# Retention attention and a two-layer MLP on one core: how the weights and the waves are loaded, and in which order two waves are computed

## Chip, cores and metric

The kernel runs on one core of a Trainium2 chip. The metric is the device time of one execution in microseconds (us). Times within the profile are counted from the start of its span. TensorE (PE) does matmuls, VectorE (DVE) and ScalarE (ACT) elementwise work, GpSimd (POOL) memsets and copies between SBUF tiles; SyncE (SP) issues DMAs, in order.

## What is computed

```python
# q, k, v: (4, 8, 768, 64) f32; lam: (8,); w_in: (512, 2048); w_out: (2048, 512); block = 64
for b in range(nb):                     # blocks of 64 positions
    intra = (qb @ kb.T) * Dmask         # Dmask[i, j] = lam ** (i - j) for i >= j, else 0
    intra = intra @ vb
    inter = (qb * lam_pow) @ kv_state   # lam_pow = lam ** (pos + 1)
    out[:, :, sl] = intra + inter
    kv_state = lam_block * kv_state + (kb * rev_pow).T @ vb
x = out.transpose(0, 2, 1, 3).reshape(3072, 512)
h = x @ w_in
g = h * (1 / (1 + exp(-1.702 * h)))
return g @ w_out                        # (3072, 512) f32
```

## The kernel before

**Waves.** The 768 positions are cut into six waves of 128. A wave holds 128 positions of all four batches, 512 rows, and all eight heads (four pairs). For each wave there is attention (with a state that goes on to the next wave), layer 1 (`mlp1`, L352: 16 blocks of 128 hidden columns, each four matmuls over the 512 model columns, followed by a `gelu` on ScalarE), and layer 2 (`mlp2`, L374: four groups of 128 rows, each 16 matmuls in four steps of `CW` = 4, followed by a copy to SBUF and a store). Matmuls are in bf16.

**Attention of waves 0 and 1** goes by units: one batch `b` and four heads `g`, eight units in all. `u_cast_kq` (L194) scales k and q by powers of lam into bf16, k on VectorE and q on GpSimd; `u_cast_v` (L208) casts v. `u_turn` (L222) transposes k and q on TensorE, `u_turn_copy` (L229) copies them from PSUM, `u_score` (L240) and `u_mask` (L249) make the masked scores, `u_out` (L278) makes the output and ScalarE copies it to `xT`, the input of layer 1; `u_kv` (L257) and `u_kv_up` (L265) update the state. **Attention of waves 2 to 5** goes by head pairs (`p_cast` L293, `p_score`, `p_mask`, `p_kv`, `p_out` L333), with the transposes done by DMAs from SyncE.

**PSUM.** The big matmuls share three buffers (`mm`); turns, outputs and states have one buffer each, scores one of two banks. Two units therefore follow each other through the same buffers.

**Loads.** q, k and v come by SyncE: `load_unit` (L78) fetches one of k, q, v of one unit, 128 KB in runs of 256 bytes; `load_pair` (L86) fetches one of them for a head pair with two DMAs. They land in tiles of the pool `ld`, two buffers per tag. The weights come by GpSimd's queue with a cast from f32 to bf16 in the DMA (`load_w_in` L159, five DMAs; `load_w_out` L165, four DMAs). `sync_behind` (L172) is a tiny DMA on SyncE that reads from the second block of `w_out`; SyncE stands at it until that block has landed. Behind it stand the 24 loads of wave 1.

**Order.** The order of the work on every engine is that in which the program writes it (`manual_schedule`). Wave 0's attention is a loop over units with three units in flight; it issues the first `w_in` load from its sixth and seventh steps. Then come all other weight loads, `sync_behind`, and wave 1's loads. After it, `main` is the list of layer-1 blocks and layer-2 steps, and `side` a list of the other pieces, each with a position in `main` before which it is written. The order of `main` is: layer 1 of wave 0, layer 2 of wave 0, then for batches 0 and 1 of wave 1 (half of its columns) layer 1 and layer 2, then the same for batches 2 and 3, then waves 2 to 5. `units1` (L480) puts wave 1's units of batches 0 and 1 into layer 2 of wave 0, with their state updates, and those of batches 2 and 3 into the work on the first half of wave 1. `full` (L514) puts wave w+1's attention into wave w's work; wave 2's lies in the second half of wave 1.

## Time and profile before

| | us |
|---|---|
| median of six runs | 225.42 |
| the six runs | 225.49, 225.97, 225.35, 223.42, 222.63, 226.01 |
| the profiled execution | 223.28 |
| its span, first to last instruction | 221.6 |
| TensorE busy in the span | 206.7 |
| VectorE, ScalarE, GpSimd busy | 92.1, 95.2, 35.2 |

TensorE's granted clock is 1.00 through the whole span. HBM reads are 27.27 MB, writes 6.29 MB. In the profile, a line of the timeline gives the start, the duration of a group of like instructions, the engine, the line of the kernel, the operation with output and inputs, how many there are, and in brackets the idle time ahead of it with what ended it. In a line of windows stand the stretch, its length, and for each of PE, PEld, DVE, ACT and POOL the busy time and number of instructions, then the granted clock, the busy share of the 16 DMA engines, and the GB/s they moved. The chain is the work that ended last, followed back from the last instruction.

### The profile page before, as it was taken

How to read it: one execution, taken by the hardware profiler on the slowest of the kernel's cores; microseconds unless marked ns; L12 is line 12 of the kernel's file. 1: busy time of each engine (PE TensorE's matmuls, PEld its weight loads, DVE VectorE, ACT ScalarE, POOL GpSimd, SP SyncE). 2: the span in 40 equal slices, each digit the busy share in tenths (PEclk: the TensorE clock that was granted, in tenths of full speed). 3: DMA queues.
4: the chain of work that ended last, by engine and by line, in shares of the span. 5: the costliest groups of instructions: out<-in, count | busy, mean ns of one | idle time of the engine just before them, and what ended most of it. 6: DMA issues, size and time to landing. Idle time of an engine off the chain costs nothing.

```text
span 221.6 us, 3886 instructions
## 1 busy us (share of the span) xinstructions
PE 206.7 (93%) x1476; PEld 108.6 (49%) x1476; DVE 92.1 (42%) x218; ACT 95.2 (43%) x202; POOL 35.2 (16%) x57
## 2 busy tenths in 40 slices
PE   7687999799999895999999999999999999999993
PEld 2354344356775584444455444554444545444452
DVE  0793000355688982182563183571363332100121
ACT  5986672273751363055612066511166411376000
POOL 4869300332121011011020120110120000000000
PEclk9999999999999999999999999999999999999999
DMA  5999999999999999889875999746792132200112
GB/s 128 238 217 145 207 206 214 218 234 218 202 215 289 190 236 134 184 240 167 195 161 140 211 250 192 179 108 187 185 264 49 27 94 71 95 3 0 47 47 95
DMA packets 109638, 35.91 MB, mean 162 GB/s; under 512 B 102324, under 2 KB 106676, under 8 KB 109620
## 3 DMA queue, kind: packets, MB, share of 16 engines
q1 hardware_dynamic: 105236, 31.47, 63.2%
q0 software_dynamic: 4240, 4.19, 12.0%
q8 instruction: 11, 0.18, 0.3%
q14 instruction: 7, 0.06, 0.1%
q10 hardware_dynamic: 144, 0.00, 0.0%
HBM read 27.27 MB, written 6.29 MB: 151 GB/s over the span
## 4 chain that ended last, share of the span: by engine, by line
PE 72%; DMA 14%; SPq 6%; DVE 2%; POOL 2%; issue 1%; ACT 0%; DVEq 0%; ACTq 0%
PE ps_out L379 32%; PE ps_h L358 29%; DMA w_out<-in_moe_w_out_dram 7%; SPq L82 5%; DMA qf<-in_q_dram 4%; PE ps_s L311 2%; DMA xT<-xs 2%; PE ps_o L337 2%; PE ps_out L397 2%; PE ps_o L339 2%; PE ps_kv L326 2%; POOL w_in L161 1%; DMA vf<-in_v_dram 1%; PE ps_t L227 1%; SPq L90 1%
## 5 line engine op out<-in xcount | busy, mean ns | idle before, releaser
L358 PE MATMUL ps_h<-xT,w_in 128*128 128x512 bf16 (+1 forms) x448 | 88.5, 349 | 1.5 <-DMA w_in<-in_moe_w_in_dram 1.5
L364 ACT ACTIVATE g_sb<-ps_h 128x512 bf16<-128x512 f32 (+1 forms) x112 | 59.5, 537 | 59.7 <-PE ps_h L358 58.7
L379 PE MATMUL ps_out<-w_out,g_sb 128*128 128x512 bf16 x368 | 84.6, 379 | 0.0
L358 PEld LDWEIGHTS <-w_in 128*128 128x128 bf16 x448 | 42.2, 98 | 38.7 <-DMA w_in<-in_moe_w_in_dram 2.1
L379 PEld LDWEIGHTS <-g_sb 128*128 128x128 bf16 x368 | 34.3, 98 | 37.3
L386 DVE COPY o_sb<-ps_out 128x512 f32<-128x512 f32 x19 | 13.1, 691 | 57.7 <-PE ps_out L379 50.2
L318 DVE TENSOR_TENSOR sm<-ps_s,dmask 128x512 bf16<-128x512 f32 x32 | 20.6, 686 | 26.9 <-PE ps_s L311 26.9
L300 POOL CAST v_sb<-vf 128x512 bf16<-128x512 f32 x16 | 11.4, 715 | 100.1 <-DMA vf<-in_v_dram 60.4
L342 ACT CAST xs<-ps_o 128x512 bf16<-128x512 f32 x16 | 9.4, 586 | 26.8 <-PE ps_o L339 23.2
L206 DVE TENSOR_TENSOR kqs<-kf,k_pow 128x256 bf16<-128x256 f32 x16 | 7.6, 477 | 26.8 <-DMA kf<-in_k_dram 22.5
L206 POOL TENSOR_TENSOR kqs<-qf,q_pow 128x256 bf16<-128x256 f32 x16 | 10.3, 648 | 28.7 <-DMA qf<-in_q_dram 26.0
L251 DVE TENSOR_TENSOR sm<-ps_s,dmask 128x512 bf16<-128x512 f32 x16 | 11.0, 689 | 3.7 <-PE ps_s L246 3.2
L329 DVE SCALAR_TENSOR_TENSOR kv<-kv,blk_pow,ps_kv 64x256 bf16<-64x256 bf16 x24 | 11.4, 476 | 0.2
L337 PE MATMUL ps_o<-kv,kq 128*128 128x128 bf16 x64 | 9.0, 220 | 2.4 <-ACT xs L342 2.4
L289 ACT CAST xT<-ps_o 128x256 bf16<-128x256 f32 x16 | 6.0, 374 | 9.7 <-PE ps_o L287 9.6
L339 PEld LDWEIGHTS <-sm 128*128 128x128 bf16 x128 | 7.9, 98 | 4.0 <-issue 2.6
L298 DVE TENSOR_SCALAR kqs<-kf,k_pow 128x256 bf16<-128x256 f32 x32 | 9.8, 348 | 0.2
L274 DVE SCALAR_TENSOR_TENSOR kv<-kv,blk_pow,ps_kv 64x64 bf16<-64x64 bf16 x32 | 7.7, 279 | 5.0 <-PE ps_kv L262 4.5
L298 DVE TENSOR_SCALAR kqs<-qf,q_pow 128x256 bf16<-128x256 f32 x32 | 9.7, 346 | 0.0
L227 PE MATMUL ps_t<-ident,kqs 128*128 128x128 bf16 x64 | 6.8, 221 | 2.8 <-DVE kqs L206 2.1
L211 ACT CAST v_sb<-vf 128x256 bf16<-128x256 f32 x16 | 6.4, 401 | 6.2 <-DMA vf<-in_v_dram 6.0
L339 PE MATMUL ps_o<-v_sb,sm 128*128 128x64 bf16 x128 | 9.0, 193 | 0.0
(54 smaller groups left out, 110.9 us busy)
## 6 DMA issues: line engine op xcount, KB each, us to landing
kf<-in_k_dram SPq DMA_DIRECT2D x48, 128.0 KB, 3.0
qf<-in_q_dram SPq DMA_DIRECT2D x48, 128.0 KB, 3.1
vf<-in_v_dram SPq DMA_DIRECT2D x48, 128.0 KB, 3.0
out_dram<-o_sb SPq DMA_DIRECT2D x23, 256.0 KB, 2.8
w_out<-in_moe_w_out_dram POOLq DMA_DIRECT2D x4, 512.0 KB, 15.8
w_in<-in_moe_w_in_dram POOLq DMA_DIRECT2D x3, 512.0 KB, 9.4
w_in<-in_moe_w_in_dram POOLq DMA_DIRECT2D x2, 256.0 KB, 5.8
kq<-kqs SPq DMA_TRANSPOSE x16, 3.5
```

The costliest lines, as they stand in the source:

```text
L82: nc.sync.dma_start(out=loaded[w, nm, b][:, 2 * g : 2 * g + 2, :, :].rearrange("s p h d -> s (p h) d"), in_=SRC[nm][b, 4 * g : 4 * g + 4, ...
L206: eng.tensor_tensor(out.rearrange("s p h d -> s (p h) d"), xf.rearrange("s p h d -> s (p h) d"), tab, op=MUL)
L298: nc.vector.tensor_scalar(kqs[:, i, :, h, :], loaded[w, "kq"[i], p][:, :, h, :], scalar1=(k_pow, q_pow)[i][:, 2 * p + h : 2 * p + h + 1], ...
L300: nc.gpsimd.tensor_copy(v_sb[w % 2][:, p, :, 0:3:2, :], loaded[w, "v", p])
L318: nc.vector.tensor_tensor(sm[:, h], s[:, h], dmask[:, h, p : p + 1, :].to_broadcast([P, B, P]), op=MUL)
L329: nc.vector.scalar_tensor_tensor(new[hd(h), p, :, hd(h)], old[hd(h), p, :, hd(h)], blk_pow[hd(h), 2 * p + h : 2 * p + h + 1], t[hd(h), :, ...
L337: nc.tensor.matmul(o[:, b, :], kq_of[w, p][:, 1, b, :], kv_sb[w % 2][:, p, b, :], start=True, stop=True)
L339: nc.tensor.matmul(o[:, b, hd(h)], sm[:, h, b, :], v_sb[w % 2][:, p, b, 2 * h, :], start=False, stop=True, skip_group_check=True)
L358: nc.tensor.matmul(t[:, bs[0] * P : bs[1] * P], w_in_sb[j][:, kc, i * P : (i + 1) * P], xT(w)[:, kc, bs[0] : bs[1], :].rearrange("p b t -> ...
L364: nc.scalar.activation(g_tile(w)[:, fc, c], h_ps.pop((w, fc))[:, c], GELU)
L379: nc.tensor.matmul(t, g_of[w][:, fc, g * P : (g + 1) * P], w_out_sb[j][:, fc % CW, :], start=(fc == 0), stop=(fc == FFC - 1))
L386: nc.vector.tensor_copy(o, t)
```

## The change

All f32 loads, the weights too, go through SyncE's queue into one ring of 26 slots of 256 KB (52 half slots; a unit load takes a half, a head pair or a weight block a whole). `coming` lists the loads in the order in which they will be used; `pump` issues those at its head as long as their slots are free in program order; `read` frees a slot. A weight block is 128 rows by 512 columns; VectorE casts it to bf16 (`cast_w`), 16 casts for `w_in` and 16 for `w_out`. The GpSimd weight loads, `sync_behind` and the pool `ld` go. The order of loads is: wave 0, `w_in`, half A of wave 1 (batches 0 and 1), `w_out`, half B (batches 2 and 3), wave 2.

The order of `main` becomes: layer 1 of wave 0, layer 1 of half A of wave 1, layer 2 of wave 0, layer 1 of half B, layer 2 of wave 1, then waves 2 to 5 as before. Half A's units lie in the last blocks of layer 1 of wave 0 (a unit every 1.3 blocks; v is cast on GpSimd, turns are copied by VectorE), half B's in layer 2 of wave 0 (every 2.2 steps; v cast and turns copied by ScalarE). The state updates of A and B are split off (`states1`) and come later: A's in layer 2 of wave 0, B's in layer 1 of half B. The casts of `w_out` are written behind A's units at every 0.6 of a position, so on VectorE 14 of them stand ahead of A's first state update and all 16 ahead of B's first cast. Wave 2's attention lies in layer 2 of wave 1.

```diff
+    NR = 26
+    ring = const.tile([P, 2 * NR, W // 2], f32, name="ring")
+    head, used, where, coming = [0], set(), {}, []
+    def load_w(kind, j, r):
+        def go(x):
+            if kind == "in":
+                src = moe_w_in[r * P : (r + 1) * P, j * W : (j + 1) * W]
+            else:
+                src = moe_w_out[(j * CW + r) * P : (j * CW + r + 1) * P, :]
+            nc.sync.dma_start(out=x, in_=src)
+            loaded[kind, j, r] = x
+        coming.append((2, (kind, j, r), go))
+    def pump():
+        while coming:
+            n, key, go = coming[0]
+            i = (head[0] + (n - 1) * (head[0] % 2)) % (2 * NR)
+            if any(c in used for c in range(i, i + n)):
+                break
+            used.update(range(i, i + n))
+            where[key] = (i, n)
+            head[0] = i + n
+            coming.pop(0)
+            go(ring[:, i : i + n, :].rearrange("s n c -> s (n c)"))
+    def read(*key):
+        i, n = where.pop(key)
+        used.difference_update(range(i, i + n))
+        return loaded.pop(key)
+    def cast_w(kind, j, r, eng):
+        eng.tensor_copy((w_in_sb if kind == "in" else w_out_sb)[j][:, r, :], read(kind, j, r))
...
+    A_UNITS = [(b, g) for g in range(NG) for b in range(HB)]
+    B_UNITS = [(b, g) for g in range(NG) for b in range(HB, B)]
+    for u in ROWS:
+        load_w("in", *u)
+    for u in A_UNITS:
+        for nm in "kqv":
+            load_unit(1, nm, *u)
+    for u in ROWS:
+        load_w("out", *u)
+    for u in B_UNITS:
+        for nm in "kqv":
+            load_unit(1, nm, *u)
+    load_full(2)
+    pump()
...
-        for j in range(1, len(IN_COLS)):
-            load_w_in(j)
-        for j in range(NJ):
-            load_w_out(j)
-        sync_behind(w_out_sb[1])
-        for u in UNITS:
-            for nm in "kqv":
-                load_unit(1, nm, *u)
+        for u in ROWS[2:]:
+            cast_w("in", *u, nc.vector)
+            pump()
...
+        for fc in range(3, FFC):
+            put(1, fc_whole, 0, fc)
+        units1(A_T, A_UNITS, A_S, nc.gpsimd, nc.vector)
+        for fc in range(3):
+            put(0.25, mlp1, 1, fc, [0, 1], HA)
+        for fc in range(3):
+            put(0.25, fc_rest, 1, fc, HA)
+        for fc in range(3, FFC):
+            put(0.5, fc_whole, 1, fc, HA)
+        for n, u in enumerate(ROWS):
+            at(13.2 + 0.6 * n, cast_w, "out", *u, nc.vector)
+        e = clock[0]
+        for j in range(NJ):
+            for g in range(3):
+                put(1, mlp2, 0, g, j)
+        for j in range(NJ):
+            put(1, mlp2, 0, 3, j)
+        states1(e + 0.5, A_UNITS, 2.2)
+        units1(e + 2, B_UNITS, 2.2, nc.scalar, nc.scalar)
+        e = clock[0]
+        for fc in range(FFC):
+            put(0.5, fc_whole, 1, fc, HB_)
+        states1(e + 1, B_UNITS, 1.9)
+        for g in range(G):
+            for j in range(NJ):
+                put(1, mlp2, 1, g, j)
+        full(e + 2, e + 8.3, 2, 2.4)
+        load_spread(e + 8, 3, 2)
```

`put` appends a piece to `main` at the running position and moves it on by its length; `at` appends to `side`.

## The prediction, on record before the changed kernel ran

> **What bounds the kernel now.** I read the page first, then TensorE's timeline from the end of wave 0's attention to the start of wave 2's layer 1, then SyncE's, then the windows for DMA rates. "Layer 1" is `mlp1`, "layer 2" is `mlp2`, a "unit" one batch and four heads of a wave.
>
> The page: busy time, and the chain of work that ended last.
>
> ```profile
> PE 206.7 (93%) x1476; PEld 108.6 (49%) x1476; DVE 92.1 (42%) x218; ACT 95.2 (43%) x202; POOL 35.2 (16%) x57
> ...
> PE 72%; DMA 14%; SPq 6%; DVE 2%; POOL 2%; issue 1%; ACT 0%; DVEq 0%; ACTq 0%
> ```
>
> TensorE holds 72% of the chain; DMA and SyncE's queue hold 20%, so at most some 44 us could be theirs, and the timeline says how much of it TensorE really loses.
>
> ```profile
> 18.29 0.27 PE L262 MATMUL ps_kv<-v_sb,kqs 128*128 128x128 bf16 x2
> 19.61 1.04 PE L358 MATMUL ps_h<-xT,w_in 128*128 128x512 bf16 x4 [1.04 <-DMA w_in<-in_moe_w_in_dram]
> ...
> 24.09 10.53 PE L358 MATMUL ps_h<-xT,w_in 128*128 128x512 bf16 x48 [0.41 <-DMA w_in<-in_moe_w_in_dram]
> 34.46 5.34 PE L379 MATMUL ps_out<-w_out,g_sb 128*128 128x512 bf16 x24
> 41.09 0.29 PE L227 MATMUL ps_t<-ident,kqs 128*128 128x128 bf16 x2 [1.29 <-DVE kqs L206]
> 41.59 0.29 PE L227 MATMUL ps_t<-ident,kqs 128*128 128x128 bf16 x2 [0.21 <-POOL kqs L206]
> ...
> 56.10 0.40 PE L227 MATMUL ps_t<-ident,kqs 128*128 128x128 bf16 x4 [0.53 <-DVE kqs L206]
> ...
> 87.41 0.22 PE L337 MATMUL ps_o<-kv,kq 128*128 128x128 bf16 x1 [2.41 <-ACT xs L342]
> ...
> 94.77 8.80 PE L358 MATMUL ps_h<-xT,w_in 128*128 128x512 bf16 x40
> ```
>
> The brackets are idle time. A matmul of 512 columns takes 0.216 us (48 of them fill 24.09 to 34.46). From 24.09 to 94.77 lie 240 such matmuls' worth (48 left of layer 1, 64 of layer 2, 128 for wave 1), 51.8 us; wave 1's eight units at 0.88 (turns 0.22, scores 0.22, outputs 0.33, states 0.11, the steps of the timeline) are 7.0; wave 2's attention is 4.45 (the steady waves start at 94.93 and 127.03 in the chain, 32.10 apart, less 27.65 for 128 matmuls). That is 63.3 of 70.7 us: **7.4 us are lost there**, 0.7 more between 19.61 and 24.09. After 94.77 TensorE has no hole to the end.
>
> SyncE's timeline shows the origin: it stands until the second block of `w_out` lands, and only then fetches wave 1.
>
> ```profile
> 12.29 1.61 SPq L82 DMA_DIRECT2D vf<-in_v_dram  x3
> 34.24 0.75 SPq L173 DMA_DIRECT2D behind<-w_out  x1
> 35.03 0.39 SPq L82 DMA_DIRECT2D kf<-in_k_dram  x1
> ```
>
> The windows (last two columns: DMA share, GB/s) give rates: loads of 256-byte runs, the casting weight loads, stores of 2 KB runs.
>
> ```profile
> 6.00:14.00 8.00, 5.89 (x63) 3.27 (x63) 7.03 (x15) 7.65 (x24) 6.10 (x9) 1.00 1.07 241
> 26.00:34.00 8.00, 8.00 (x38) 3.63 (x37) 0.00 (x0) 5.58 (x10) 0.00 (x0) 1.00 1.24 206
> 204.00:214.00 10.00, 10.00 (x48) 4.56 (x47) 1.38 (x2) 0.60 (x1) 0.00 (x0) 1.00 0.14 52
> ```
>
> **The one unknown: microseconds per weight row block of 256 KB (call it r).** The new loads are f32, 2 KB runs, on SyncE. Fast end: the casting loads write 206 GB/s of bf16, so read 412 GB/s of f32, r = 0.64. Slow end: 241 GB/s, r = 1.09. Nearest row: stores on the same queue with the same 2 KB runs, 52 / 0.14 = 371 GB/s at a full share, r = 0.70, which I take. SyncE's issue does not set it (0.33 to 0.45 us for a 256 KB store).
>
> **Part by part, with r = 0.70.**
>
> Start. SyncE's 24 loads of wave 0 stay as they are, to 13.9. A unit load lands 3.0 us after issue, and they run 0.55 apart, so weight row n lands at about 16.5 + 0.70(n+1): rows 0, 7, 15 at 17.2, 22.1, 27.7. VectorE is busy with wave 0 to 18.76 and then casts. A cast of 128x512 is not in the trace: L298's 0.347 us for half as many elements is the low bound, the 0.69 of L386 (512 elements from PSUM) the high one; I take 0.48, nearer L298, which reads SBUF. Rows 0 and 1 are cast at 19.7, where layer 1 started before (19.61): 0. Rows 2 and 3 at 20.7 (they were needed at 21.33), rows 4 to 7 at 22.7, and 16 matmuls end at 23.5. So block 1 starts at 23.5, not 24.09: **gain 0.6**. At 0.69 per cast it would be 24.3. Later blocks arrive every 2.8 us and are used every 3.46, so the casts stay hidden.
>
> Layer 1 with half A of wave 1. A's 12 loads follow at 0.55: the first unit's q lands at 28.8, GpSimd's 0.61 makes 29.4. TensorE reaches that unit's turn after 28 matmuls, 23.5 + 6.05 = 29.55: just in time. Units come every 1.65 us by load and every 2.0 by use. TensorE: 10.4 (48 matmuls) + 3.1 (four units at 0.77, states come later) + 6.9 (layer 1 of half A) = 20.4. New holes, since the first unit's score follows its turn without a matmul between (turn to score is 1.03 us at 7.62 to 8.65 in wave 0, less the turn's 0.22): 0.8; the fourth's score behind a turn and an output: 0.5; layer 1 of A right behind the last output, which needs a ScalarE copy (0.37 and hand-overs): 0.7. Plus 0.4 for the switches that the present units also show (four matmuls take 0.95 instead of 0.86 beside a score). Layer 2 starts at 46.3.
>
> Layer 2 of wave 0. `w_out` follows A (last landing 34.3) and is in at 45.5; its casts lie on an idle VectorE. A new order matters: VectorE's state updates of unit A0 stand behind 14 of the 16 `w_out` casts, and unit A1's state matmul (49.0) waits for them; row 13 lands at 44.1, plus 1.5 for cast and four updates: 45.6, hidden by 3.4 us. B's loads land from 46 to 52.1; its first turn is at 50.0, the fourth near 57. So 13.8 + 0.44 (states) + 3.1 (units) + 1.0 for holes and switches: 64.6. Its end carries no load wait.
>
> The rest. Second half of layer 1, 6.9 + 0.44: 72.0. Wave 2's loads land by 65.3, while its last cast comes at about 71; its transposes stand on SyncE behind wave 0's four stores, which are issued by 65. Layer 2 of wave 1 with wave 2's attention: 13.8 + 4.45 = 18.3: 90.3. Here 28 matmuls (6.0 us) follow the last output and cover its copy (0.59) and transpose (2.6): the 2.41 us hole goes. From wave 2's layer 1 on the order is that of before: 0.
>
> GpSimd loses the nine weight issues (6.9 us, off the path). Beside VectorE's f32 SBUF casts its own casts stretch (1.59 instead of 0.62 us at 163.06); two such stretches on its memsets (1.03 and 1.88) still end before 28.8: 0. SBUF writes grow by 4.2 MB; this is inside r.
>
> **Sum:** 94.77 - 90.3 = **4.5 us** less. The profiled execution took 223.28 (span 221.6 and 1.7 around it), so 218.8; the six runs lie in two bunches (222.63 to 223.42, 225.35 to 226.01), their median 225.42 is 2.1 above the profiled run and their mean is 224.8. I forecast from the mean, since this trace does not show what parts the bunches: **220.3**.
>
> A rule that speaks against the change. The row first: unit loads land 3.0 us after issue and still follow each other every 0.55 us, so the fixed cost of one overlaps the others, and the sum above goes by that. The Trainium skill, "DMA: Bandwidth & Descriptors", section Measured, asks for 1 MiB and more per DMA, and its fit gives each DMA 2.0 us plus its bytes at 436 GB/s. Taken one at a time, that is by estimate 2.6 us per row block, and by the stall formula of rival 1 a kernel some 30 us slower.
>
> **Rivals.**
>
> 1. *Slow loads (slower).* 2 KB loads run at the 241 GB/s of the unit loads. Every row later delays A: TensorE's stall at its first turn is 16(r - 0.70) - 0.15, at r = 1.09 6.1 us; row 13 of `w_out` then lands at 23.1 + 30r = 55.8, 57.3 with its updates, against 55.1: 2.2 more. 220.3 + 8.3 = **228.6**. It eats the whole gain from r = 0.99 (265 GB/s) on. For: loads have never run faster on this queue in the trace. Against: those were 256-byte runs, at SyncE's issue pace (128 KB per 0.55 us).
> 2. *Tight units (no change).* The spacing of A and B leaves one or no matmul block between a unit's dependent steps, and each of eight units loses the 0.81 us of turn to score: 6.5 instead of the 3.0 counted (2.0 in A, 1.0 in B): **223.8**. For: wave 0, so interleaved, takes 1.45 us per unit for 0.88 of work. Against: in A and B four matmuls stand between most of the steps.
> 3. *No holes.* All the 3.4 us of holes and switches counted in A and B hide: **216.9**. For: nothing is late by more than 0.8. Against: the orders named leave nothing to run in them.
>
> **How the numbers follow.** The forecast 0.60, with casts from 0.35 to 0.69, r from 0.64 to 0.85 (2.3 us at the top) and the two bunches, its own range 217.5 to 222.8; no holes 0.08; tight units 0.16; slow loads 0.16. About 1% is what a measurement of this kernel tells from no change: 223.2 to 227.7. Tight units fall below that line one time in eight (0.02). Faster 0.60 + 0.08 + 0.02 = 0.70; same 0.14; slower 0.16. The range 216.5 to 226.5 holds the forecast, tight units, half of no holes and a fifth of slow loads, about 0.83.
>
> **What would show it.** Right: weight rows landing about 0.7 us apart; TensorE's idle before the first A turn under 0.5 us; no DMA named in its waits after 24 us; layer 2 of wave 0 starting near 46, wave 2's layer 1 near 90; 32.1 us per wave after it. Wrong: row 15 landing after 30, a state matmul waiting for VectorE near 49, or later waves longer than 32.1, which would mean that the ring or the shared queue delays them.

## The result and the profile after

The changed kernel takes 226.80 us (median of 35 runs, 224.63 to 230.58) against 224.23 us of the kernel before (70 runs, 222.63 to 226.90): ratio 1.0096, 95% interval 1.0073 to 1.0118. It is about 1% slower; 220.3 was forecast. The profiled execution took 227.24 us, its span is 225.5 us. Executions that were over 1.5% above the fastest of the same kernel, most of them at a lower granted clock, are left out of every ratio (so 1.0096 is not 226.80 / 224.23), and of e1, e9, e11 and e16 only such an execution was profiled, so that their starts are missing in the table below and of e16 only the places of SyncE's work are read.

The page of the changed kernel, busy time and chain:

```profile
PE 209.8 (93%) x1476; PEld 110.2 (49%) x1476; DVE 106.9 (47%) x250; ACT 94.2 (42%) x198; POOL 30.8 (14%) x52
...
PE 79%; SPq 7%; DMA 6%; DVE 4%; issue 1%; ACT 1%; ACTq 0%; DVEq 0%
```

DMA fell from 14% of the chain to 6%, TensorE rose from 72% to 79%, and still the kernel is longer. A share of the chain says who was waited for last, not that time was saved. TensorE's timeline says where the time lies (changed kernel; start, duration, idle time ahead in brackets):

```profile
20.06 0.38 PE L386 MATMUL ps_h<-xT,w_in 128*128 128x512 bf16 x1 [0.56 <-ACT xT L317]
20.87 1.46 PE L386 MATMUL ps_h<-xT,w_in 128*128 128x512 bf16 x3 [0.43 <-DVE w_in L137]
...
31.98 0.39 PE L255 MATMUL ps_t<-ident,kqs 128*128 128x128 bf16 x4
...
48.76 1.03 PE L407 MATMUL ps_out<-w_out,g_sb 128*128 128x512 bf16 x4
...
66.73 1.04 PE L386 MATMUL ps_h<-xT,w_in 128*128 128x256 bf16 x8
...
93.65 0.81 PE L386 MATMUL ps_h<-xT,w_in 128*128 128x512 bf16 x3
95.89 8.14 PE L386 MATMUL ps_h<-xT,w_in 128*128 128x512 bf16 x37 [1.43 <-DMA xT<-xs]
...
110.46 0.40 PE L340 MATMUL ps_s<-kq 64*128 64x128 bf16 x8 [3.17 <-DVE sm L347]
111.34 0.38 PE L355 MATMUL ps_kv<-v_sb,kqs 128*128 128x128 bf16 x4 [0.48 <-DVE kv L358]
...
131.11 1.24 PE L386 MATMUL ps_h<-xT,w_in 128*128 128x512 bf16 x5
```

Wave 2's layer 1 starts at 93.65, 1.1 us earlier than before (94.77). But wave 2 then lasts to 131.11, 37.5 us instead of 32.1: it first waits for its own last `xT`, then for wave 3's first masks. So a gain of 1.1 is followed by a loss of 5.4, of which the three waits in brackets (1.43, 3.17 and 0.48) are 5.1. From wave 3 on the two kernels run alike.

Why the masks are late stands in VectorE's timeline of the changed kernel. The first lines are casts of `w_in` and half A's first cast. The line at 67.99 is half B's first state update, with wave 2's first cast behind it. The last ones are casts of wave 3's last head pair (L327) and wave 3's first masks (L347):

```profile
20.38 0.43 DVE L137 CAST w_in<-ring 128x512 bf16<-128x512 f32 x1 [0.49 <-DMA ring<-in_moe_w_in_dram]
21.03 0.43 DVE L137 CAST w_in<-ring 128x512 bf16<-128x512 f32 x1 [0.22 <-DMA ring<-in_moe_w_in_dram]
...
29.91 0.43 DVE L137 CAST w_in<-ring 128x512 bf16<-128x512 f32 x1 [0.34 <-DMA ring<-in_moe_w_in_dram]
30.50 0.42 DVE L234 TENSOR_TENSOR kqs<-ring,k_pow 128x256 bf16<-128x256 f32 x1 [0.16 <-DMA ring<-in_k_dram]
...
67.99 0.97 DVE L302 SCALAR_TENSOR_TENSOR kv<-kv,blk_pow,ps_kv 64x64 bf16<-64x64 bf16 x4 [5.45 <-PE ps_kv L290]
68.99 0.62 DVE L327 TENSOR_SCALAR kqs<-ring,k_pow 128x256 bf16<-128x256 f32 x2
...
103.87 0.70 DVE L327 TENSOR_SCALAR kqs<-ring,k_pow 128x256 bf16<-128x256 f32 x2 [4.52 <-DMA ring<-in_k_dram]
107.48 0.35 DVE L327 TENSOR_SCALAR kqs<-ring,q_pow 128x256 bf16<-128x256 f32 x1 [2.92 <-DMA ring<-in_q_dram]
108.76 0.35 DVE L327 TENSOR_SCALAR kqs<-ring,q_pow 128x256 bf16<-128x256 f32 x1 [0.93 <-DMA ring<-in_q_dram]
109.03 1.28 DVE L347 TENSOR_TENSOR sm<-ps_s,dmask 128x512 bf16<-128x512 f32 x2
```

VectorE stands 4.52, 2.92 and 0.93 us for wave 3's last loads, and the masks that TensorE wants stand behind those casts in its order. SyncE's timeline of the changed kernel shows where these loads stand (L96 are loads, L331 and L372 transposes):

```profile
14.53 10.13 SPq L109 DMA_DIRECT2D ring<-in_moe_w_in_dram  x16
...
33.68 10.07 SPq L109 DMA_DIRECT2D ring<-in_moe_w_out_dram  x16
...
65.88 1.01 SPq L96 DMA_DIRECT2D ring<-in_v_dram  x2
...
70.20 7.79 SPq L331 DMA_TRANSPOSE kq<-kqs  x4
78.04 1.15 SPq L96 DMA_DIRECT2D ring<-in_k_dram  x2
...
92.85 1.22 SPq L372 DMA_TRANSPOSE xT<-xs  x1
...
98.54 1.88 SPq L331 DMA_TRANSPOSE kq<-kqs  x1
100.47 1.13 SPq L96 DMA_DIRECT2D ring<-in_k_dram  x2
101.71 1.24 SPq L331 DMA_TRANSPOSE kq<-kqs  x1
103.06 2.40 SPq L96 DMA_DIRECT2D ring<-in_q_dram  x2
```

The weights take 20.2 us of SyncE, as long as it stood before for `w_out`, and wave 2's last load is issued at 65.88, where it was 64.55 before. Wave 3's first load comes at 78.04 (73.02 before), behind four transposes. Its last loads, k at 100.47 and q at 103.06, stand behind transposes of wave 3 itself (98.54 and 101.71). In the kernel before all of wave 3's loads are out before its first transposes; the last two groups there:

```profile
95.82 1.05 SPq L90 DMA_DIRECT2D vf<-in_v_dram  x2
...
97.86 2.65 SPq L302 DMA_TRANSPOSE kq<-kqs  x2
```

The diff has this order. `load_spread(e + 8, 3, 2)` writes the last three of wave 3's twelve loads at positions 26, 28 and 30 from the start of half B's layer 1, while wave 2 starts at 24 and wave 3's casts, each followed by its transpose, stand at 25, 27, 29 and 31. The kernel before writes all twelve ahead of wave 2 (positions 52 to 78.4 of `main`, where wave 2 starts at 80).

The windows of the changed kernel around the start of layer 1 (the last three columns: granted clock, DMA share, GB/s):

```profile
18.00:20.00 2.00, 1.13 (x12) 0.70 (x12) 1.38 (x2) 1.91 (x7) 1.61 (x1) 1.00 0.97 334
20.00:22.00 2.00, 1.51 (x4) 0.47 (x5) 1.18 (x3) 0.42 (x3) 0.00 (x0) 0.59 0.99 367
22.00:24.00 2.00, 2.00 (x11) 1.18 (x10) 1.33 (x4) 0.52 (x2) 0.00 (x0) 0.56 1.05 357
```

The loads of weights run at 357 and 367 GB/s, near the 371 of the forecast. But TensorE, busy for 1.13 of 2 us, is granted 0.59 and 0.56 of its clock in the next four: by estimate (0.41 + 0.44) x 2 = 1.7 us of matmuls are lost there.

### The profile page after: what moved, and what is told of

The parts are those of the page before. It is cut to its first block, busy times and chain, and to the rows that moved or that the text cites. A ratio compares the mean times of both kernels' runs of the same rounds, so it can differ in the third digit from the quotient of the medians.

```text
span 225.5 us, 3971 instructions
## 1 busy us (share of the span) xinstructions
PE 209.8 (93%) x1476; PEld 110.2 (49%) x1476; DVE 106.9 (47%) x250; ACT 94.2 (42%) x198; POOL 30.8 (14%) x52
## 4 chain that ended last, share of the span: by engine, by line
PE 79%; SPq 7%; DMA 6%; DVE 4%; issue 1%; ACT 1%; ACTq 0%; DVEq 0%
PE ps_h L386 35%; PE ps_out L407 33%; SPq L86 6%; DMA ring<-in_moe_w_in_dram 2%; DMA ring<-in_q_dram 2%; PE ps_s L340 2%; PE ps_o L368 2%; PE ps_o L366 2%; PE ps_out L425 2%; PE ps_kv L355 2%; DMA xT<-xs 1%; DVE sm L347 1%; PE ps_t L255 1%; PE ps_o L315 1%; DVE kv L358 1%
## 5 line engine op out<-in xcount | busy, mean ns | idle before, releaser
L407 PE MATMUL ps_out<-w_out,g_sb 128*128 128x512 bf16 x368 | 85.6, 379 | 0.0
L386 PEld LDWEIGHTS <-w_in 128*128 128x128 bf16 x448 | 42.9, 98 | 39.8 <-issue 3.0
L347 DVE TENSOR_TENSOR sm<-ps_s,dmask 128x512 bf16<-128x512 f32 x32 | 20.6, 686 | 22.6 <-PE ps_s L340 22.5
L329 POOL CAST v_sb<-ring 128x512 bf16<-128x512 f32 x16 | 11.8, 739 | 101.7 <-DMA ring<-in_v_dram 66.2
L234 POOL TENSOR_TENSOR kqs<-ring,q_pow 128x256 bf16<-128x256 f32 x16 | 10.6, 665 | 35.8 <-DMA ring<-in_q_dram 20.6
L327 DVE TENSOR_SCALAR kqs<-ring,k_pow 128x256 bf16<-128x256 f32 x32 | 10.4, 363 | 5.0 <-DMA ring<-in_k_dram 4.8
L327 DVE TENSOR_SCALAR kqs<-ring,q_pow 128x256 bf16<-128x256 f32 x32 | 10.0, 348 | 4.4 <-DMA ring<-in_q_dram 4.2
L340 PE MATMUL ps_s<-kq 64*128 64x128 bf16 x128 | 6.4, 218 | 3.5 <-DVE sm L347 3.5
L234 DVE TENSOR_TENSOR kqs<-ring,k_pow 128x256 bf16<-128x256 f32 x16 | 7.5, 467 | 4.5 <-ACT k_pow L185 4.2
L246 PE MATMUL ps_f<-zeros 128*128 128x512 bf16 x20 | 8.4, 544 | 1.3 <-DVE zeros L169 1.3
L137 DVE CAST w_in<-ring 128x512 bf16<-128x512 f32 x16 | 7.2, 448 | 4.0 <-DMA ring<-in_moe_w_in_dram 4.0
```

The lines of the kernel that those rows point to most:

```text
L234: eng.tensor_tensor(kqs_of[w, b][:, i, gs(g)].rearrange("s p h d -> s (p h) d"), xf, tab, op=MUL)
L327: nc.vector.tensor_scalar(kqs[:, i, :, h, :], x[:, :, h, :], scalar1=(k_pow, q_pow)[i][:, 2 * p + h : 2 * p + h + 1], scalar2=None, op0=MUL)
L329: nc.gpsimd.tensor_copy(v_sb[w % 2][:, p, :, 0:3:2, :], read(w, "v", p))
L347: nc.vector.tensor_tensor(sm[:, h], s[:, h], dmask[:, h, p : p + 1, :].to_broadcast([P, B, P]), op=MUL)
L386: nc.tensor.matmul(t[:, bs[0] * P : bs[1] * P], w_in_sb[fc // CW][:, kc, (fc % CW) * P : (fc % CW + 1) * P], xT(w)[:, kc, bs[0] : bs[1], : ...
L407: nc.tensor.matmul(t, g_of[w][:, fc, g * P : (g + 1) * P], w_out_sb[j][:, fc % CW, :], start=(fc == 0), stop=(fc == FFC - 1))
```

## The experiments

For orientation, the starts of layer 1 of waves 2 and 3 in the profiled execution of each kernel (TensorE's timelines), and the ratio to the kernel before with its interval.

| kernel | wave 2 | wave 3 | between | ratio |
|---|---|---|---|---|
| before | 94.77 | 126.86 | 32.1 | 1 |
| changed | 93.65 | 131.11 | 37.5 | 1.0096 (1.0073 to 1.0118) |
| e1 wave 3's loads earlier | | | | 1.0129 (1.0059 to 1.0200) |
| e2 filler matmuls | 93.62 | 131.31 | 37.7 | 1.0098 (1.0052 to 1.0144) |
| e3 both | 95.25 | 133.81 | 38.6 | 1.0167 (1.0109 to 1.0225) |
| e4 wave 3's casts later | 94.56 | 132.79 | 38.2 | 1.0132 (1.0065 to 1.0199) |
| e5 loads of waves 3 to 5 on GpSimd | 98.52 | 133.87 | 35.4 | 1.0342 (1.0276 to 1.0408) |
| e6 stores on GpSimd | 94.78 | 129.62 | 34.8 | 1.0090 (1.0049 to 1.0130) |
| e7 before, without the wait | 96.25 | 128.34 | 32.1 | 1.0041 (1.0001 to 1.0081) |
| e8 the new order alone | 105.44 | 141.04 | 35.6 | 1.0641 (1.0580 to 1.0702) |
| e9 loads by hand | | | | 1.0347 (1.0295 to 1.0398) |
| e10 e9 and fillers | 95.13 | 134.89 | 39.8 | 1.0347 (1.0299 to 1.0394) |
| e11 e9 and stores on GpSimd | | | | 1.0365 (1.0304 to 1.0426) |
| e12 before, wave 3's loads later | 92.15 | 126.17 | 34.0 | 0.9990 (0.9960 to 1.0020) |
| e13 wave 2's attention earlier | 96.93 | 134.56 | 37.6 | 1.0313 (1.0259 to 1.0368) |
| e14 e13 and loads by hand | 97.93 | 130.25 | 32.3 | 1.0107 (1.0081 to 1.0133) |
| e15 e14 and fillers | 97.82 | 129.91 | 32.1 | 1.0102 (1.0056 to 1.0148) |
| e16 half of w_out's loads | | | | 1.0185 (1.0119 to 1.0250) |
| e17 e15, wave 2's loads split | 97.09 | 129.19 | 32.1 | 1.0030 (0.9986 to 1.0073) |
| e18 e17, and the start | 95.89 | 127.98 | 32.1 | 1.0023 (0.9986 to 1.0060) |

### The loads, the clock and the casts, each alone (e1 to e4)

e1 and e3:

```diff
-        load_spread(e + 8, 3, 2)
+        load_spread(e + 4, 3, 1.6)
```

e2 and e3 (in the loop over wave 0's units, ahead of its last matmuls):

```diff
+            if i == N:
+                fill(2)
...
             if i == N + 1:
+                fill(4)
```

e4:

```diff
-                full(e + 1, e + 10, w + 1, 3.0)
+                full(e + (5 if w == 2 else 1), e + 10, w + 1, 3.0, 3.0 if w == 2 else 2.0)
```

> The changed kernel with one edit: wave 3's loads are written from 4 positions after the start of half B's layer 1, 1.6 apart, instead of from 8, 2.0 apart. Theory: wave 2 takes 37.5 us instead of 32.1 because wave 3's loads come so late on SyncE that VectorE, which works in order, stands at wave 3's casts (waits of 4.5 and 2.9 us for k and q) with wave 3's first masks behind them; TensorE then loses 3.2 us to the mask and 1.4 us to a transpose queued behind loads. So wave 2 goes to 32 to 33.5 us and the time falls by 4 to 5 us, to 222 from 226.8. Rival A: the loads are late because the ring has no free slot for them or the DMA engines are full; then loads written earlier land no earlier and the time stays within 1 us. Rival B: earlier loads push wave 2's own transposes back on SyncE, and what wave 2 gains the end of wave 1 loses: layer 1 of wave 2 starts 2 us or more after 93.7.

> The changed kernel with six more matmuls on zeros: two behind the last unit's score of wave 0 and four ahead of the first layer-1 matmul. Theory: the granted clock of 0.59 and 0.56 from 20 to 24 us (mean 0.992) follows from TensorE standing in 18 to 20 us (1.13 of 2.0 us busy) while the first weight rows land; with work there the clock stays at 1.00, layer 1 of wave 0 ends 1.7 us sooner, the mean clock is 0.999 or more and the time falls by 1.5 to 2 us, to about 225. Rival: the clock falls for another reason (what ran some microseconds earlier, or chance of the run); then the clock stays at 0.985 to 0.992 in most runs and the time is the same or up to 1 us longer, for the matmuls added.

> The changed kernel with both edits, wave 3's loads earlier and the six matmuls on zeros. If the two losses are separate, the gains add: 5.5 to 7 us, so 220 to 221, which is below the kernel before (224.2) by about 1.5%. If they share a cause or the first only moves the wait on, less than the larger of the two.

> The changed kernel with the loads where they are, but wave 3's four casts written at 66, 69, 72 and 75 instead of 62, 64, 66 and 68, so that the masks of its first two head pairs stand ahead of the third and the fourth cast on VectorE. Theory (VectorE in order is what carries the late loads to TensorE): the 3.2 us wait of the second score for the first mask falls below 1 us, and the time by 2 to 3 us. Rival (the data itself is too late for the attention of wave 3, whatever VectorE's order): TensorE waits as long, at a later score, and the time changes by less than 1 us.

e1 took 228.49 us, 1.3% above the kernel before, and e3 228.35: no gain, where 222 and 220 to 221 were expected. Rival B had the mechanism: now all of wave 3's loads stand ahead of wave 2, the wait for the masks is gone, and the one for `xT` has grown. TensorE's timeline of e3:

```profile
95.25 0.81 PE L386 MATMUL ps_h<-xT,w_in 128*128 128x512 bf16 x3
99.54 5.70 PE L386 MATMUL ps_h<-xT,w_in 128*128 128x512 bf16 x13 [3.48 <-DMA xT<-xs]
```

Wave 2's last `xT` transpose had its input at 92.62 but was issued at 96.07, behind the third transpose, two pair loads and a store: the wait has changed places on the same queue. The 13 matmuls behind it took 5.70 us, twice the time of 13 at the full clock (2.8).

e2 (227.62 us) asks whether the low clock cost time. Its windows in the same stretch:

```profile
20.00:22.00 2.00, 1.75 (x12) 0.82 (x11) 1.31 (x4) 0.48 (x3) 0.00 (x0) 1.00 1.04 387
22.00:24.00 2.00, 2.00 (x12) 0.93 (x10) 1.30 (x4) 1.78 (x6) 0.00 (x0) 1.00 0.91 276
```

The clock stays at 1.00 here, and layer 2 of wave 0 starts at 48.74 instead of 48.76: the 1.7 us were no loss of their own. That the six matmuls kept the clock is not shown. In e6 and e13, which lack them and have the changed kernel's program up to there, TensorE was busy for 1.15 and 1.17 of 2.00 us and the clock stayed at 1.00 too; their layer 2 starts at 49.04 and 48.79. The time of e2 did not fall by the 1.5 to 2 us expected, and its clock dropped later, to 0.50 and 0.69 from 110 to 114 us. TensorE is at half A's first turn at 31.20 instead of 31.98, but there it waits for the k cast (0.53), which comes no earlier (30.71, against 30.50), and then for the q cast (0.56): half A's loads set the pace.

e4 (227.73) took away the place of the masks behind the casts, and TensorE waited for the data itself. Its waits (us in total, times, longest):

```profile
PE ps_s L340 <- DMA kq<-kqs: 4.0, 2, 2.4
...
PE ps_h L386 <- DMA xT<-xs: 1.9, 1, 1.9
```

So wave 3's loads are late for TensorE too, and not only for VectorE's order, as the rival had it.

### Relief for SyncE (e5, e6) and the parts of the change (e7, e8)

e5, e6 and e7 (on the kernel before):

```diff
-                nc.sync.dma_start(
+                (nc.gpsimd if w > 2 else nc.sync).dma_start(
...
-            nc.sync.dma_start(out=out[r0 : r0 + P, :], in_=o)
+            (nc.gpsimd if w < NW - 1 else nc.sync).dma_start(out=out[r0 : r0 + P, :], in_=o)
...
-        sync_behind(w_out_sb[1])
```

e8 (the weights as in the kernel before, with no casts on VectorE):

```diff
-        for u in ROWS[2:]:
-            cast_w("in", *u, nc.vector)
-            pump()
...
+            if i == N - 2:
+                load_w_in(0, 0, 2)
+            if i == N - 1:
+                load_w_in(0, 2, 4)
+        for j in range(1, NJ):
+            load_w_in(j)
+        nc.sync.dma_start(out=behind, in_=w_in_sb[1][0:1, 0, 0:2])
+        for u in A_UNITS:
+            for nm in "kqv":
+                load_unit(1, nm, *u)
...
```

> After, with one edit: the pair loads of waves 3, 4 and 5 are issued by GpSimd instead of SyncE; the ring, the order and everything else stay. Theory now (one in-order queue): wave 2 is 37.5 us long instead of 32.1 because SyncE issues weights, waves, stores and transposes one behind the other from 44 to 113 us, so that wave 2's xT transpose and wave 3's loads come late. With wave 3's loads on another queue PE's wait for xT (1.43 us) and for the first masks (3.17 and 0.48) go, wave 2 takes 32 to 33.5 us, and the time is 219.5 to 222.5, ratio 0.975 to 0.99. Rival (the 16 DMA engines themselves are full between 60 and 110 us): loads land as late as before, from the other queue too, waves 2 is 36 to 38 us, and the time is 226 to 228. In between (waits of VectorE for loads gone, but GpSimd's loads land among the transposes and slow these): 223 to 225.

> After, with one edit: the output stores of waves 0 to 4 are issued by GpSimd instead of SyncE. If the wait of SyncE in its order matters (a store stands until its rows are computed, the loads behind it too), this frees some 0.45 us of issue for each of eight stores ahead of wave 3's last loads, and what SyncE stands at them: wave 2 gets 1 to 3 us shorter than 37.5, the time is 224 to 226, ratio 0.99 to 1.0 against the kernel before. If it is only the mass of the loads and transposes, or the 16 DMA engines, the time stays at 226.5 to 228.

> The kernel before with one edit: the tiny DMA that held SyncE until the second block of w_out had landed (13.9 to 34.2 us) is left out, so that wave 1's loads follow wave 0's at once; weights still come by GpSimd with the cast in the DMA. Theory (SyncE is the scarce thing; those 20 us of idleness are what the change spent on the weights): wave 1's and wave 2's loads come earlier, the waits for them go, and the time falls to 221 to 224 if the weights do not suffer. Rival (contention: the weights share the 16 engines with wave 1's loads and arrive later): layer 1 of wave 0 waits 2 to 6 us for w_in, and the time is 226 to 231.

> The new order of work alone: after, but the weights come as before, by GpSimd's DMAs with the cast in them, with no casts on VectorE; SyncE waits for the second block of w_in, then loads half A, half B and wave 2 through the ring. Theory (the weights' 20.2 us of issue on SyncE took what the new order had won): SyncE is some 14 to 20 us ahead at wave 2's loads, wave 2's layer 1 starts at 89 to 92 us, wave 2 takes 32 to 33 us, the time is 217.5 to 222. Rival (the order itself is at fault: half A's and half B's pieces stand in each other's way): wave 2's layer 1 starts at 93 to 95 us and the time is 223.5 to 228. If wave 3's loads still come late although SyncE is ahead, wave 2 stays at 35 to 38 us and the time is 222 to 225.

e5 took 232.51 us, worse than either theory had it. Its list of DMA issues (median us from issue to landing last):

```profile
ring<-in_v_dram POOLq DMA_DIRECT2D x24, 128.0 KB, 6.1
kq<-kqs SPq DMA_TRANSPOSE x16, 5.1
```

In the changed kernel loads land 3.5 us after issue and these transposes 3.5 us. With the loads on the second queue both took longer, and the DMA share rose from 0.91 and 0.84 to 1.20 and 1.26 in 70 to 80 and 80 to 90 us. TensorE then waited for `kq` (1.52), `xs` (2.23) and `xT` (1.42 and 1.52).

e6 took 226.16 us, no different from the changed kernel (ratio 1.0090 against 1.0096) and between its two expectations, though its parts moved: wave 2 was 2.6 us shorter and started 1.1 later.

e7 (224.87) shows that leaving out the wait alone gains the kernel before nothing. Without it wave 1's loads go out beside those of the weights, TensorE waits 1.50, 1.48 and 1.05 us for `w_in` (1.04 and 0.41 before), and the time is 0.4% longer, between the two expectations.

e8 (239.14) was to show the new order without the loads of weights on SyncE. TensorE's timeline of e8:

```profile
34.24 0.40 PE L256 MATMUL ps_t<-ident,kqs 128*128 128x128 bf16 x2 [2.81 <-DVE kqs L235]
37.86 0.39 PE L256 MATMUL ps_t<-ident,kqs 128*128 128x128 bf16 x2 [3.22 <-POOL kqs L235]
...
44.41 0.40 PE L256 MATMUL ps_t<-ident,kqs 128*128 128x128 bf16 x2 [3.43 <-DVE kqs L235]
```

TensorE stands 9.5 us for half A's loads: e8 holds SyncE until 25.18 for the second block of `w_in`, and they come beside the casting loads of `w_out`. My theory (that the weights' issue on SyncE had eaten the gain) expected 217.5 to 222 us. Since e8 brings a wait of its own, it does not tell what the new order alone is worth. But the later waits are there without any weights on SyncE: 1.66 us for `xT`, 1.08 and 0.48 for the masks, wave 2 35.6 us long.

### The order of SyncE, in both kernels (e9 to e12)

e9, and in e10 with e2's fillers, in e11 with wave 1's stores on GpSimd:

```diff
-        load_spread(e + 8, 3, 2)
+        for n, t in enumerate([1.0, 1.2, 3.0, 5.0, 7.0, 8.6, 9.6, 10.6, 12.5, 13.5, 15.5, 17.2]):
+            at(e + t, load_pair, 3, "kqv"[n % 3], n // 3)
```

e12, on the kernel before:

```diff
-                            side.append((m + 4 + 2.4 * (3 * p + i), (load_pair, w + 2, nm, p)))
+                            side.append((m + (11.6 if w == 1 else 4) + 2.4 * (3 * p + i), (load_pair, w + 2, nm, p)))
```

> After, with one edit: the twelve pair loads of wave 3 (24 DMAs) are placed by hand in SyncE's order, where it stood (before and between wave 2's four kq transposes, and between the outputs), the last before wave 2's last xT transpose, instead of every second position to 16 us into wave 2. Theory now (what counts is each DMA's place in SyncE's order: in after wave 2's last xT transpose was issued 1.8 us after its input was ready, behind a load and a store, and wave 3's last loads only at 103 to 110 us): PE's wait for xT falls from 1.43 to under 0.5 us, the one for the first masks from 3.17 + 0.48 to under 0.6, wave 2 takes 32 to 33.5 us instead of 37.5, the time is 221.5 to 223.5, ratio 0.985 to 0.997. Rival (the 16 DMA engines cannot do more before 110 us, as the loads on GpSimd's queue made the transposes slower, 5.1 us instead of 3.5): the kq transposes land late, wave 2's scores wait at 76 to 82 us by 2 to 5 us, the time stays at 225.5 to 228.

> The last kernel's loads placed by hand, and with it six matmuls of zeros, two and four, in the gaps of TensorE at the end of wave 0's attention (18 to 20 us; they add nothing to any output). Alone the six matmuls kept the granted clock at 1.00 through 20 to 24 us but gained nothing, since TensorE waited for loads later. If those waits are gone now, the 1.8 us that half clock cost stay gained: 1 to 2 us below the kernel with the loads placed alone, 220 to 222.5, ratio 0.98 to 0.992. Rival: wave 2's layer 1 starts at the same time as without them, since the loads and transposes set it; then no difference within 0.5 us.

> The loads of wave 3 placed by hand, and wave 1's four output stores on GpSimd's queue, so that they stand before no transpose and no load of SyncE. If SyncE's order still holds something back: 0.3 to 1.5 us less than with the loads by hand alone. If not: the same within 0.5 us; if GpSimd's v casts for wave 3 then stand behind stores that wait for outputs, up to 1 us more.

> The mirror of this in the kernel before: wave 3's pair loads are put 7.6 positions later, which makes SyncE's order between wave 2's kq transposes and wave 3's the same as in after; nothing else is touched. Theory (this order is what makes wave 2 long in after): PE's wait of 3 to 4 us for wave 3's first masks appears in this kernel too, wave 2 takes 35 to 37 us, and the time is 226 to 228.5, ratio 1.01 to 1.02. Rival (in after the loads are late because the weights and the earlier work have filled SyncE and the DMA engines; in before there is room): wave 2 stays at 32 to 33.5 us, and the time at 224 to 225.

e9 took 231.40 us, e10 231.37, e11 232.40: 3.5 to 3.7% slower. e9 is slower than either side had expected; the fillers and the moved stores gain nothing, as their rivals had it. In e10 SyncE issues from 69.56 to 102.20 almost without a pause, the last `xT` transpose at 97.38 instead of 92.85, and TensorE waits for it (timeline of e10):

```profile
97.22 0.38 PE L386 MATMUL ps_h<-xT,w_in 128*128 128x512 bf16 x1 [1.49 <-DMA xT<-xs]
101.06 10.53 PE L386 MATMUL ps_h<-xT,w_in 128*128 128x512 bf16 x37 [3.46 <-DMA xT<-xs]
```

e12 is the mirror, and the theory lost it as well. Wave 3's last three loads now stand behind its first transposes as in the changed kernel, and the kernel before does not get slower (223.08 us, ratio 0.9990; 226 to 228.5 was expected). TensorE's timeline of e12:

```profile
92.15 8.80 PE L358 MATMUL ps_h<-xT,w_in 128*128 128x512 bf16 x40
105.51 0.40 PE L311 MATMUL ps_s<-kq 64*128 64x128 bf16 x8 [1.31 <-DVE sm L318]
```

The wait for wave 3's masks does appear (1.31, and wave 2 takes 34.0 instead of 32.1 us), but wave 2 starts 2.6 us earlier, since the hole of 2.41 us that the kernel before had ahead of its last output is gone. Loads of wave 3 and transposes of wave 2 share one queue in both kernels; which of them goes first decides where TensorE waits. What also differs is how far ahead of TensorE the queue is. In e12 the last `xT` transpose goes out at 87.42, 4.7 us before wave 2; in the changed kernel at 92.85, 0.8 us before it.

### Wave 2's attention, or the mass of DMA work (e13 to e18)

Two causes were left: (a) wave 2's attention, which the change puts into layer 2 of wave 1, too close to wave 2; (b) DMA work as such. e13 moves the attention up; e14 also places wave 3's loads around it, and e15 adds the fillers:

```diff
-        full(e + 2, e + 8.3, 2, 2.4)
+        full([e - 2, e - 0.5, e + 5.5, e + 7.2], e + 5.3, 2, 2.4)
...
-        load_spread(e + 8, 3, 2)
+        for n, t in enumerate([2.5, 3.5, 4.5, 6.5, 9.5, 12, 14.5, 16.5, 17.5, 18.5, 19.8, 20.8]):
+            at(e + t, load_pair, 3, "kqv"[n % 3], n // 3)
```

e16 loads only half of `w_out` and casts each row block twice:

```diff
-    for u in ROWS:
-        load_w("out", *u)
+    for j, r in ROWS:
+        if r % 2 == 0:
+            load_w("out", j, r)
```

> After, with wave 2's attention moved up: its first two casts come at the end of layer 2 of wave 0, before half B's state updates, the other two in half B's layer 1, and its scores and outputs start 3 positions earlier, so that 28 matmuls (some 6.4 us) instead of 16 follow the last output. Wave 3's loads keep their places. Cause (a): PE's wait of 1.43 us for xT goes, its wait for wave 3's masks (3.17 us) stays or shrinks by 1 to 2 as the transposes no longer stand among the loads; wave 2 takes 33 to 35 us, the time is 222.5 to 225, ratio 0.99 to 1.003. Cause (b): the kq transposes are no earlier than 70 to 77 us by SyncE, PE waits for them at 72 to 80 us, by 2 to 5 us; the time stays at 226 to 229.

> The last kernel, and wave 3's loads placed by hand around the moved transposes: seven pairs before wave 2's last xT transpose, five behind it, all before wave 2's layer 1. Cause (a): no wait for xT and none for the masks over 0.6 us, wave 2 takes 32 to 33.5 us, the time is 221 to 223.5, ratio 0.985 to 0.997. Cause (b): as with the loads by hand alone, transposes land late, 227 to 232.

> The last kernel and the six matmuls of zeros that keep TensorE's clock at 1.00 through 20 to 24 us (they add nothing to any output). Cause (a): with the later waits gone the 1.8 us stay gained, 219.5 to 222, ratio 0.98 to 0.99. Cause (b): no difference to the last kernel within 0.5 us.

> After, with only every second row block of w_out loaded (eight DMAs instead of sixteen, 2.1 MB and some 5 us of SyncE and of the DMA engines less); each is cast twice, so half of w_out's rows are replaced by others and the output is not the reference's, while TensorE, VectorE and ScalarE do the same work. Cause (b): half B's and wave 2's loads come 5 us earlier, wave 2's transposes and wave 3's loads too, the time falls by 3 to 5 us to 222 to 224. Cause (a): wave 2's transposes still wait for casts behind half B's state updates, so that nothing from 70 us on moves; 226 to 227.5.

e16 (228.58 us) leaves out eight of the loads. SyncE's timeline of e16:

```profile
61.20 1.00 SPq L96 DMA_DIRECT2D ring<-in_v_dram  x2
...
70.30 7.80 SPq L337 DMA_TRANSPOSE kq<-kqs  x4
78.15 1.15 SPq L96 DMA_DIRECT2D ring<-in_k_dram  x2
```

SyncE is done with wave 2's loads 4.7 us earlier (61.20, not 65.88), and at 70 us nothing has moved (70.20 and 78.04 in the changed kernel), as cause (a) said; the time lies above its 226 to 227.5. SyncE is held there by wave 2's casts, which stand behind half B's state updates on VectorE, and these follow TensorE: in the changed kernel VectorE stands 5.45 us for the state matmul, updates the state at 67.99 and casts at 68.99. So the loads of weights are not what makes wave 2's transposes late.

e13 (230.43) shows the trade once more: the wait for `xT` goes, as (a) said, but one for `kq` comes at 75 us, as (b) said, and the masks stay late. Its time lies above both ranges. TensorE's timeline of e13:

```profile
74.78 0.40 PE L340 MATMUL ps_s<-kq 64*128 64x128 bf16 x8 [2.90 <-DMA kq<-kqs]
...
112.24 0.40 PE L340 MATMUL ps_s<-kq 64*128 64x128 bf16 x8 [2.77 <-DVE sm L347]
```

Only with both moved (e14, 225.97; e15, 225.61) are `xT` and masks in time, and wave 2 is 32.3 and 32.1 us long, as cause (a) said. But it starts 4.3 and 4.2 us later than in the changed kernel, so wave 3 starts only 0.9 and 1.2 earlier, and the ratios (1.0107, 1.0102) are no better than 1.0096. The times that (a) forecast (221 to 223.5, and 219.5 to 222) are missed, and e15 differs from e14 by less than 0.5 us, which was (b)'s forecast. So (a) against (b) is not decided. One wait was left, here in TensorE's timeline of e14:

```profile
75.48 0.61 PE L340 MATMUL ps_s<-kq 64*128 64x128 bf16 x8 [3.48 <-DMA kq<-kqs]
```

Wave 2's first transpose is issued at 70.17, behind all of wave 2's loads and three stores. e17 writes the loads of pairs 2 and 3 behind the transposes' casts of pairs 0 and 1; e18 also loads half A's first unit ahead of the last four row blocks of `w_in` (whose casts come after that unit's) and makes half B's state updates earlier:

```diff
-    load_full(2)
+    for p in range(2):
+        for nm in "kqv":
+            load_pair(2, nm, p)
...
-        full([e - 2, e - 0.5, e + 5.5, e + 7.2], e + 5.3, 2, 2.4)
+        full([e - 7.5, e - 5.8, e + 5.5, e + 7.2], e + 5.3, 2, 2.4)
+        for n, t in enumerate([-7.4, -7.3, -7.2, -5.7, -5.6, -5.5]):
+            at(e + t, load_pair, 2, "kqv"[n % 3], 2 + n // 3)
...
-        states1(e + 1, B_UNITS, 1.9)
+        states1(e + 0.3, B_UNITS, 1.5)
```

> The last kernel with fillers, and one more move: the loads of wave 2's pairs 2 and 3 are written behind the casts and transposes of pairs 0 and 1, which come some 5 positions earlier, so that on SyncE the first two transposes stand ahead of twelve loads and two or four stores. If the wait of 2.21 us at 75.6 us is only the place of the first transpose in SyncE's order, it goes to under 0.5 us, no other wait over 1 us takes its place, and the time is 221 to 223.5, ratio 0.985 to 0.998 against the kernel before. If wave 2's last two transposes or wave 3's loads then come late instead (SyncE has no room left in the whole stretch), a wait of 2 to 4 us comes back at 80 to 112 us and the time stays at 224.5 to 227.

> The last kernel with two more moves: half A's first three loads stand ahead of the last four row blocks of w_in on SyncE, and the casts of these four behind that unit's cast and copy on VectorE; half B's state updates come earlier and closer (every 1.5 positions from 0.3, all ahead of wave 2's first scores). If the waits of 0.69, 0.53, 0.51 and 1.14 us that these remove were real losses, wave 2's layer 1 starts at 94 to 95.5 us, wave 2 takes 32.1, and the time is 221.5 to 223.5, ratio 0.985 to 0.997 against the kernel before. If TensorE, being earlier, only meets the next late thing (half A's later units, half B's loads), the start stays at 96 to 97.5 and the time at 224 to 226, ratio 1.0 to 1.008.

e17 took 225.16 us, e18 224.66, ratios 1.0030 and 1.0023 with 1 inside both intervals: as fast as the kernel before, and not faster; both had hoped for less than 223.5. In e17 no DMA is named in TensorE's waits after 44 us. In e18 the removed waits made wave 2 start 1.2 us earlier, and a new one of 1.26 us for `kq` came at 82.07. No version beat the kernel before.

## Why the prediction was wrong, point by point

**Rates of the loads: right.** Casts of weight rows follow each other every 0.65 us (20.38, 21.03); 0.70 was forecast. A cast takes 0.43 us, forecast 0.48. Rival 1 (slow loads) is out.

**"weight row n lands at about 16.5 + 0.70(n+1)": the offset was wrong.** Row 1 was to land at 17.9 and row 15 at 27.7; VectorE waited for them until 20.38 and 29.91, 2.5 and 2.2 us later. The sum took the 3.0 us from issue to landing of a unit load; a weight load on the same queue lands 5.4 us after issue (list of DMA issues). Half A's first k cast stands behind row 15's cast, and TensorE reached the first turn of A at 31.98 instead of 29.55: 2.4 us. The low clock at 20 to 24 us looked like the cause. But at the full clock TensorE comes to that turn at 31.20 and 31.46 (e2, e13) and has waited there for that cast (0.53 and 0.67 us), and layer 2 starts no earlier.

**Half A, layer 2 of wave 0, half B: right.** From the first turn to layer 2 it is 16.8 us (16.75 forecast), layer 2 of wave 0 takes 18.0 (18.3), half B's layer 1 7.7 (7.4). Rival 2 (tight units) is out.

**"Here 28 matmuls (6.0 us) follow the last output": a misreading.** In the trace 16 follow (90.19 to 93.65, 3.5 us). The last output's copy ends at 91.02, its transpose is issued at 92.85 behind a load and a store, and TensorE waits 1.43 us after three matmuls of wave 2. The position of that output (19.1 of 24) was in the diff; it leaves four steps of four matmuls. Layer 2 of wave 1 with the attention took 19.3 us instead of 18.3.

**"From wave 2's layer 1 on the order is that of before: 0": this step failed.** Its price was 5.4 of the 8.4 us by which the span (225.5) is off the sum (221.6 - 4.5 = 217.1). In its place the runs show two waits. TensorE waits for wave 3's masks (3.17 and 0.48), because the order is not that of before: the last three of wave 3's loads stand behind wave 2's first block and behind wave 3's own transposes; with all of them ahead (e3) this wait goes. And it waits for the last `xT` (1.43), whose transpose stands behind a load and a store; with wave 2's attention earlier (e13) this wait goes.

Why neither remedy saves time is argued, not shown: SyncE has no room there. Eight transposes at 1.2 us, twelve pair loads at 1.1 and four stores at 0.45 make, by estimate, 25 us of SyncE. They begin with wave 2's casts, which follow half B's state updates and so TensorE itself (e16), and from SyncE's first transpose to wave 2's layer 1 there are 23.5 us in the changed kernel (70.20 to 93.65), 27.0 in the kernel before (67.74 to 94.77) and 27.8 in e14 (70.17 to 97.93). The forecast checked that wave 2's loads came early and stopped there; it did not follow the queue through the transposes to wave 3's loads. It did name the sign to look for: "later waves longer than 32.1, which would mean that the ring or the shared queue delays them". It is the queue. The ring does hold loads back up to wave 2's last one, which goes out only when the eighth cast of `w_out` has been written; but with wave 3's loads at most 18 of the 52 half slots are taken, and each of these is issued at the position at which it is written. None of the three rivals was this; the one on the slow side was another mechanism.

**What the experiments settle.** The added 5.4 us are not the weights' issue on SyncE (e8, e16), not the stores alone (e6 takes off 2.6), not the place of wave 3's loads alone (e3, e10), and not the place of wave 2's attention alone (e13). Wave 2 is as short as before only when attention, transposes and loads are moved together (e14, e15: 32.3 and 32.1 us), and then most of the 5.4 us stands ahead of wave 2 instead. Another queue for the loads does not help (e5). The Trainium skill, "DMA: Bandwidth & Descriptors", section Issuing engines are not separate DMA queues, states that DMAs from several engines end up on the same 16 DMA engines and that only the time of issuing is saved, usually a small one. e5 fits the first half (transposes land after 5.1 instead of 3.5 us). The second half is too mild for this case: SyncE spends 1.0 us on the two loads of a pair and 1.2 us on a transpose, and in e10 that fills it for over 30 us.

**What stays open.** e18 has no wait over 1.3 us, and its wave 2 starts at 95.89 where 90.3 was forecast. By stages: its first turn of A comes at 31.01 (1.5 later than forecast); from there to layer 2 18.4 us (1.7 more); layer 2 of wave 0 18.9 (0.6 more); from half B to wave 2 27.5 (1.8 more). TensorE's waits that the trace names from 21 us on sum to 5.2 us, and 3.4 us of holes and switches were in the forecast already. Whether a placement without them exists was not tried.

## What to carry to other kernels

When a change brings work forward, follow each in-order queue past the place where the change ends: the waves behind may seem to be "in the order of before" and still be late, because the queue that feeds them has another order or less room than before. A wait that moves when one of two neighbours on a queue is moved (e3, e10, e12, e13) is a sign that the queue has no room there: add up what it must issue between two points in time before moving anything on it. Here moving the whole chain only moved the time ahead of wave 2. And count what follows the last producer from the positions in the code, not from the neighbouring wave.

## What the hardware showed that was not expected

- The granted clock can drop without a long stand of TensorE, and no rule for it comes out of these runs. In the changed kernel waits of 0.33, 0.56 and 0.43 us, with 1.13 of 2.00 us busy, were followed by 0.59 and 0.56 of the clock for 4 us; in e6 and e13, with 1.15 and 1.17 of 2.00 us busy at the same place, it stayed at 1.00. The 3.17 us wait at 110 us was followed by 1.00 in the changed kernel; one of 1.57 us at the same place in e2 was followed by 0.50 and 0.69. The Trainium skill, "TensorE: Matmul & The Clock Gate", Part 1, puts the drop to half rate after an idle window of about 3.4 us; the two drops above came after far shorter waits.
- In the changed kernel a load of 256 KB in runs of 2 KB lands 5.3 to 5.4 us after issue (median), one of 128 KB in runs of 256 bytes 3.2 to 3.5 us, on the same queue. The same 128 KB issued by GpSimd take 5.4 to 6.1 us to land and 0.75 to 0.84 us each of GpSimd (e5).
